# Pairing attention pieces across block edges in a fused retention + feed-forward kernel

## The chip, the cores and the metric

The kernel runs on one core of one Trainium2 chip. The metric is device microseconds (us) of one execution, lower is better. The engines are TensorE (PE, with its weight loads shown as PEld), VectorE (DVE), ScalarE (ACT), GpSimd (POOL) and SyncE (SP); POOL and SP also issue the DMAs that matter here.

## The reference

Eight batches of eight heads, 576 positions, 64 features per head. For every head, scores = q k^T / 8 are multiplied by a decay, gamma^(i-j) for i >= j and 0 above the diagonal, and then by v. The result, laid out as x of 4608 tokens by 512 features, goes through a feed-forward layer:

```python
ret = scores * Dmat[None, :, :, :]
x = np.matmul(ret, v).transpose(0, 2, 1, 3).reshape(B * S, H * D)
h = x @ w_in                       # 512 -> 2048
g = h * np.clip(h + 3.0, 0.0, 6.0) / 6.0
return (g @ w_out).astype(np.float32)   # 2048 -> 512
```

## The kernel before

**Tokens and blocks.** The 4608 tokens are handled as nine blocks of 512 tokens (kb = 0 to 8). Blocks 0 to 7 hold the first 512 positions of one batch each; block 8 holds the last 64 positions of all eight batches. The attention is computed in 36 pieces of 128 tokens: four "main" pieces per batch, and four "rest" pieces (numbers 12, 21, 30 and 35), each made of the 64 last positions of two batches. Pieces 8 to 11 belong to block 2, 13 to 16 to block 3, 17 to 20 to block 4, 22 to 25 to block 5, 26 to 29 to block 6, 31 to 34 to block 7.

**Feed-forward.** For each block, GEMM1 (`gemm1`, matmuls on L400 into `ph`) runs 16 units of four 128x512 matmuls; each unit's result goes through one ACT instruction (L407) and one DVE instruction (L408) into `gt`. GEMM2 (`unit2`, `g2`, L458 into `pout`) then runs 16 units of four matmuls: four token rows (mc) of four units (part). After a row's last unit ACT copies `pout` out (L462) and SP stores it.

**Attention.** It is retention in chunks. For a piece c: `transpose_k` (L286) and `transpose_q` (L291 scales q and v on DVE, L292) make `qk_c` and `vs_c` by DMA transposes on SP's queue. `scores` or `scores_second` multiply k by q on PE (L301, L572); DVE masks the result into `at_c` (L305, L580). `inter` (L323) multiplies q by the running state `tbd`; the first piece of a batch has none. `intra` (L334) adds `at_c` times v; ACT casts the sum into the feed-forward input `xt16` (L340). `update_mm` (L358) forms the piece's contribution to the state, DVE adds and scales it (L371, L374, L375), and ACT copies it into a `tbd` buffer (L387, L388). Rest pieces only read states and update none.

**Steps.** From piece 8 on, the attention is dropped into GEMM2 by hand. `step(ended, begun)` (L585) ends the pieces of one pair (inter, intra) and begins the next pair (scores, update). Its PE order is: inter of both ended pieces, scores of both begun ones, intra of both ended ones, state updates of both begun ones. `put` (L604) runs the units in order and calls whatever stands at unit j after it; j = -1 is ahead of unit 0. During GEMM2 of block kb the pieces of block kb+1 are computed, and those of block kb+2 are transposed (`ahead`, L560). A step also asks for the loads of the pieces six further on (`load_until`; `kn` and `qv` have six buffers), on POOL's queue.

Before the change, the table `AT` (L646) places the steps, and every block starts and ends its own chain of pairs: the first step of a GEMM2 has nothing to end and the last one nothing to begin. A block of four pieces has 3 steps, one of five has 4 (the fifth piece is alone), and block 8's single piece has 2. `ahead` stands at the last four or five units of GEMM2.

**Order and buffers.** The order on each engine is the order of the code. PSUM has 8 banks: four of tag `ph` (shared by GEMM1's `ph`, GEMM2's `pout`, the second scores' two banks and the second inter's `o`), two of `sc`, one of `o` and one of `tu` (state updates). `qk` and `vs` have six buffers each, `at` four, `tbd` five.

Of the kernel before, what the change touches and what calls it, by code (L numbers as in the profile page):

```python
# [11 lines left out]
FP16 = mybir.dt.float16  # L12
# [5 lines left out]
def kernel(  # L18
# [17 lines left out]
    B, H, S, D = q.shape  # L36
    NTOK, DM = out.shape
    DFF = moe_w_in.shape[1]
    P = 128
    NPAIR = H // 2  # L40
# [4 lines left out]
    NMB = NTOK // MBLK  # L45
# [8 lines left out]
    last_of = {}  # L54
    for b in range(B):
# [3 lines left out]
        if b >= 2 and b % 2 == 0 or b == B - 1:  # L59
            j = (b - 1) // 2  # L60
            pieces.append(("rest", j, 0, [(0, 2 * j, MAIN, HALF), (HALF, 2 * j + 1, MAIN, HALF)]))
    last_of[B] = len(pieces) - 1
    NP = len(pieces)
# [9 lines left out]
    work = ctx.enter_context(tc.tile_pool(name="work", bufs=3))  # L73
# [115 lines left out]
    st = {}  # L189
# [7 lines left out]
                later.pop(0)()  # L197

    def scale_v(c):
        vs = work.tile([P, 2, H, D], FP16, tag="vs", bufs=6, name=f"vs_{c}")  # L200
        st.setdefault(c, {})["vs"] = vs[:, 1]
        nc.vector.tensor_tensor(out=vs[:, 1], in0=loaded[c]["qv"][:, 1], in1=gqv[:, 1],  # L202
                                op=ALU.mult)

    def qk_of(c):
        if "qk" not in st.setdefault(c, {}):
            st[c]["qk"] = work.tile([P, 2, NPAIR, P], FP16, tag="qk", bufs=6, name=f"qk_{c}")
        return st[c]["qk"]

    def k_by_pe(c, tag="ph"):  # L210
        kn = loaded[c]["kn"]
        pk = psum.tile([P, NPAIR, P], FP16, tag=tag, bufs=4 if tag == "ph" else 1,
                       name=f"trk_{c}")
        for p in range(NPAIR):
            nc.tensor.transpose(pk[:, p, :], kn[:, 2 * p:2 * p + 2, :], ident16)
        nc.scalar.copy(qk_of(c)[:, 1], pk)  # L216

    def q_by_pe(c):
        q16, qk = loaded[c]["q16"], qk_of(c)
        pq = psum.tile([P, NPAIR, P], FP32, tag="ph", bufs=4, name=f"trq_{c}")  # L220
        for p in range(NPAIR):
            for h2 in range(2):
                r = slice(h2 * HALF, h2 * HALF + HALF)
                nc.tensor.matmul(pq[r, p, :], q16[:, 2 * p + h2, :], dq[:, 2 * p + h2, :],
                                 start=(p == 0), stop=(p == NPAIR - 1), skip_group_check=True)
        if c == EARLY - 1:
            for p in (0, 2):
                nc.scalar.copy(qk[:, 0, p:p + 2], pq[:, p:p + 2])
        else:
            nc.scalar.copy(qk[:, 0], pq)  # L230
# [54 lines left out]
    def transpose_k(c):  # L285
        nc.sync.dma_start_transpose(qk_of(c)[:, 1], loaded[c]["kn"].rearrange("s h d -> s (h d)"))  # L286

    def transpose_q(c):
        vs = work.tile([P, 2, H, D], FP16, tag="vs", bufs=6, name=f"vs_{c}")
        st[c]["vs"] = vs[:, 1]  # L290
        nc.vector.tensor_tensor(out=vs, in0=loaded[c]["qv"], in1=gqv, op=ALU.mult)  # L291
        nc.sync.dma_start_transpose(st[c]["qk"][:, 0], vs[:, 0].rearrange("s h d -> s (h d)"))  # L292
# [126 lines left out]
    def g1_columns(kb, fc, ph, cols):  # L419

        t0 = kb * MBLK
        for dmc in range(NCC):
            nc.tensor.matmul(ph[:, cols], win16[:, dmc, P * fc:P * fc + P],  # L423
                             xt16[:, dmc, t0 + cols.start:t0 + cols.stop],
                             start=(cols.start == 0 and dmc == 0),
                             stop=(cols.stop == MBLK and dmc == NCC - 1),
                             skip_group_check=True)
        if cols.stop == MBLK:
            g1_act(kb, ph, fc)

    def g1_first(kb):

        banks = [g1_bank(kb, fc) for fc in range(2)]
        for dmcs in ((0, 1), (2, 3)):
            for fc in range(2):
                g1_mm(kb, banks[fc], fc, dmcs)
        for fc in range(2):
            g1_act(kb, banks[fc], fc)
# [48 lines left out]
    for i in range(4):  # L487
        if i == 2:
            load(4)
        load_wout(4 * i, 4 * i + 4)  # L490

    scale_v(0)
    for c in range(EARLY):
        k_by_pe(c)
        warm(1, MBLK)
        if c == 0:
            fill_gfull()
        q_by_pe(c)
        if c == 0:
            warm(1, MBLK)  # L500
        else:
            inter(c - 1)
            intra(c - 1)
        if c < EARLY - 1:
            scores(c)
            run_later(9)
            state_early(c)
            run_later(9)
            scale_v(c + 1)
        else:  # L510
            scores_last(c)
            state_early(c)
            out_last(c)
# [9 lines left out]
    def unit1(kb, f0):  # L523
        return lambda: g1(kb, f0)

    def unit2(kb, mc, part):
        return lambda: g2(kb, mc, part)

    def first_step(c):


        old, new, b = c - 1 >= EARLY, c + 1 < 8, pieces[c - 1][1]
        if old:
            before = state_of.get(b)
            o = psum.tile([P, NPAIR, P], FP32, tag="o", name=f"o_{c - 1}")
            st[c - 1].update(o=o, first=True)
            copy = intra(c - 1, copy_later=True, more=before is not None)
            update_mm([c - 1])
            load_until(c - 1 + NBUF)
            update_state(c - 1, copies_later=True)  # L540
        if new:
            q_by_pe(c + 1)
        if old and new:
            run_later(9)
        if EARLY <= c < 8:
            scores(c, 0)
        if old and before is not None:
            for p in range(NPAIR):
                nc.tensor.matmul(o[:, p, :], tbd[before][:, p, :], st[c - 1]["qk"][:, 0, p, :],
                                 start=False, stop=(p == NPAIR - 1), skip_group_check=True)  # L550
        if new:
            k_by_pe(c + 1, "ph" if old else "tu")
        if old:
            copy()
        if c < 8:
            run_later(9)
        if EARLY <= c < 8:
            scale_v(c)

    def ahead(c):  # L560
        transpose_k(c)
        transpose_q(c)
# [41 lines left out]
    def put(units, steps):  # L604

        for do, *which in steps.get(-1, ()):
            do(*which)
        for j, unit in enumerate(units):
            unit()
            run_later(1)  # L610
            for do, *which in steps.get(j, ()):
                do(*which)

    def of_block(kb):
        return list(range(last_of[kb - 1] + 1, last_of[kb] + 1)) if kb < NMB else []

    def gemm1(kb, steps):

        units = {0: [lambda: g1_first(kb)]}.get(kb, [])
        done = {0: 2, 1: 4}.get(kb, 0)  # L620
        put(units + [unit1(kb, f) for f in range(done, NFC)], steps)
# [13 lines left out]
    for fc in range(2):  # L635
        g1_columns(1, fc, banks[fc], done)
    first_step(8)
    transpose_q(8)
    for fc, cols in ((2, done), (0, last), (1, last), (3, done), (2, last), (3, last)):
        g1_columns(1, fc, banks[fc], cols)  # L640
    gts.pop(0)


    gemm1(1, {0: [(transpose_q, 9)], 1: [(transpose_k, 10)],
              4: [(transpose_q, 10)], 5: [(transpose_k, 11)], 8: [(transpose_q, 11)]})
    AT = {1: (-1, 7), 4: (-1, 7, 12), 5: (-1, 3, 7, 11)}  # L646
    for kb in range(1, NMB - 1):
        mine, next_ = of_block(kb + 1), of_block(kb + 2)
        pairs = [mine[i:i + 2] for i in range(0, len(mine), 2)]
        steps = {}  # L650
        for j, ended, begun in zip(AT[len(mine)], [[]] + pairs, pairs + [[]]):
            steps.setdefault(j, []).append((step, ended, begun))
        for j, c in enumerate(next_, start=16 - len(next_)):
            steps.setdefault(j, []).append((ahead, c))
        put([unit2(kb, mc, part) for mc in range(MBLK // P) for part in range(4)], steps)
        gts.pop(kb)
        gemm1(kb + 1, {})
# [34 lines left out]
```

## Time and profile before

| | us |
|---|---|
| median of three runs (308.92 to 309.75) | 309.16 |
| the profiled execution's own time | 308.84 |
| its span (first to last instruction) | 307.0 |
| PE busy in the span | 298.3 (97%) |
| DVE busy | 185.8 (61%) |
| ACT busy | 174.7 (57%) |
| POOL busy | 107.9 (35%) |

The profile is one execution. The chain of waits follows the work that ended last back through whatever released each piece of it; its list in order of time gives the start, the length and the instruction group of each stretch. A stretch's length there runs to the start of the next one, so lengths add up. Timelines of one engine instead give each group's own duration, in which pipelined instructions overlap a little. Times are us from the start of the span. The granted TensorE clock was 0.998 of full speed.

### The profile page before, as it was taken

What the parts mean: (1) busy time and instruction counts of PE and PEld (TensorE: products, weight loads), DVE (VectorE), ACT (ScalarE), POOL (GpSimd) and SP (SyncE); (2) the same over time, 40 slices, a digit from 0 to 9 for tenths busy, and PEclk for the clock granted to TensorE, in tenths of its full rate; (3) what the DMA queues carried; (4) which work ended last, traced back from release to release, by engine and by line L of the source; (5) the groups of instructions that cost most, each with busy time, mean ns of one, the idle gap of its engine ahead of it and who ended that gap; (6) DMA issues with size and microseconds to landing.
All of it is one profiled execution on the core that took longest, in us unless ns stands there. A gap on an engine that the chain in (4) does not pass through costs nothing.

```text
span 307.0 us, 5776 instructions
## 1 busy us (share of the span) xinstructions
PE 298.3 (97%) x2239; PEld 150.1 (49%) x2239; DVE 185.8 (61%) x309; ACT 174.7 (57%) x301; POOL 107.9 (35%) x134
## 2 busy tenths in 40 slices
PE   6999998999999999999999999999999999999994
PEld 2654455544544554445545544455445544444443
DVE  4768336795858872885587738856787357207700
ACT  5568346783667455744574638544765467228611
POOL 8963577636630590055233830257000000000000
PEclk9999999999999999999999999999999999999999
DMA  9999999999999899659999996099920120010022
GB/s 68 147 200 205 190 167 204 169 132 153 158 160 165 85 137 157 106 35 161 167 137 94 139 184 136 4 166 140 141 70 36 68 68 2 34 68 36 1 68 68
DMA packets 153163, 35.51 MB, mean 116 GB/s; under 512 B 143792, under 2 KB 148656, under 8 KB 153136
## 3 DMA queue, kind: packets, MB, share of 16 engines
q0 software_dynamic: 117264, 18.36, 84.6%
q1 hardware_dynamic: 35472, 16.26, 25.7%
q10 hardware_dynamic: 400, 0.52, 0.5%
q8 instruction: 17, 0.28, 0.4%
q14 instruction: 10, 0.08, 0.1%
HBM read 36.70 MB, written 9.44 MB: 150 GB/s over the span
## 4 chain that ended last, share of the span: by engine, by line
PE 83%; DMA 8%; POOL 5%; ACT 2%; DVE 1%; issue 0%; POOLq 0%; ACTq 0%
PE pout L458 37%; PE ph L400 35%; DMA wout<-in_moe_w_out_dram 4%; DMA qv<-in_q_dram 4%; PE o L334 3%; POOL qv L91 2%; PE sc L301 2%; PE o L323 2%; PE u L358 1%; POOL kn L91 1%; POOL win L95 1%; PE pout L471 1%; PE sc L572 1%; PE ph L423 1%; ACT qk L216 0%
## 5 line engine op out<-in xcount | busy, mean ns | idle before, releaser
L408 DVE SCALAR_TENSOR_TENSOR gt<-u,ph 128x512 f16<-128x512 f32 x144 | 98.1, 688 | 63.6 <-ACT u L407 62.9
L458 PE MATMUL pout<-wout,gt 128*128 128x512 f16 x560 | 126.0, 379 | 0.0
L400 PE MATMUL ph<-xt,win 128*128 128x512 f16 x560 | 122.3, 379 | 0.2 <-DVE gt L408 0.2
L407 ACT ACTIVATE u<-ph,cb 128x512 f32<-128x512 f32 x144 | 98.3, 688 | 25.4 <-PE ph L400 24.2
L400 PEld LDWEIGHTS <-win 128*128 128x128 f16 x560 | 54.7, 98 | 66.0 <-issue 0.4
L458 PEld LDWEIGHTS <-gt 128*128 128x128 f16 x560 | 52.7, 98 | 60.8
L91 POOL DMA_DIRECT2D kn<-in_k_dram x40 | 34.5, 865 | 91.8 <-PE u L358 72.6
L462 ACT COPY osb<-pout 128x512 f32<-128x512 f32 x35 | 20.5, 587 | 48.9 <-PE pout L458 48.5
L305 DVE TENSOR_TENSOR at<-sc,mask_wide 128x1024 f16<-128x1024 f32 x19 | 23.2, 1223 | 27.6 <-PE sc L301 27.4
L91 POOL DMA_DIRECT2D qv<-in_q_dram x40 | 34.2, 861 | 6.4 <-DMA wout<-in_moe_w_out_dram 3.3
L91 POOL DMA_DIRECT2D qv<-in_v_dram x40 | 34.6, 870 | 2.8 <-DMA wout<-in_moe_w_out_dram 1.7
L387 ACT COPY tbd<-ts 64x256 f16<-64x256 f16 x28 | 11.4, 406 | 32.7 <-DVE ts L371 16.9
L340 ACT CAST xt<-o 128x512 f16<-128x512 f32 x35 | 19.4, 589 | 6.4 <-PE o L334 4.0
L291 DVE TENSOR_TENSOR vs<-qv,gqv 128x1024 f16<-128x1024 f16 x28 | 18.0, 686 | 3.3 <-DMA qv<-in_v_dram 3.3
L580 DVE TENSOR_TENSOR at<-sc,mask_wide 128x512 f16<-128x512 f32 x24 | 15.4, 682 | 0.0
L334 PE MATMUL o<-at,vs 128*64 128x128 f16 x280 | 12.4, 225 | 1.1 <-ACT xt L340 1.0
L388 ACT COPY tbd<-ts 64x256 f16<-64x256 f16 x28 | 11.3, 403 | 0.4
L334 PEld LDWEIGHTS <-vs 128*64 128x64 f16 x280 | 8.9, 111 | 4.4 <-DVE vs L202 2.1
L374 DVE TENSOR_TENSOR ta<-u,ts 128x256 f32<-128x256 f32 x21 | 8.8, 417 | 3.1 <-PE u L358 3.1
L375 DVE TENSOR_TENSOR ts<-ta,gc 128x256 f16<-128x256 f32 x21 | 8.9, 426 | 1.7
L301 PE MATMUL sc<-qk 64*128 64x128 f16 x184 | 9.6, 226 | 0.4 <-ACT qk L230 0.3
L323 PEld LDWEIGHTS <-tbd 128*128 128x128 f16 x112 | 7.0, 98 | 4.0
(69 smaller groups left out, 117.7 us busy)
## 6 DMA issues: line engine op xcount, KB each, us to landing
out_dram<-osb SPq DMA_DIRECT2D x32, 256.0 KB, 4.1
kn<-in_k_dram POOLq DMA_DIRECT2D x32, 128.0 KB, 4.6
qv<-in_q_dram POOLq DMA_DIRECT2D x32, 128.0 KB, 5.0
qv<-in_v_dram POOLq DMA_DIRECT2D x32, 128.0 KB, 5.7
wout<-in_moe_w_out_dram POOLq DMA_DIRECT2D x4, 512.0 KB, 15.4
win<-in_moe_w_in_dram POOLq DMA_DIRECT2D x3, 512.0 KB, 10.1
win<-in_moe_w_in_dram POOLq DMA_DIRECT2D x2, 256.0 KB, 6.1
kn<-in_k_dram POOLq DMA_DIRECT2D x8, 64.0 KB, 4.5
```

Of the source, the lines that this page charges most:

```text
L91: nc.gpsimd.dma_start(dst[p0:p0 + n], src[b, :, s0:s0 + n, :].rearrange("h s d -> s h d"))
L291: nc.vector.tensor_tensor(out=vs, in0=loaded[c]["qv"], in1=gqv, op=ALU.mult)
L301: nc.tensor.matmul(sc[:, h2, p, :], qk[r, 1, p, :], qk[r, 0, p, :], start=True, stop=True)
L305: later.append(lambda: nc.vector.tensor_tensor(out=at.rearrange("t a b s -> t (a b) s"), in0=sc.rearrange("t a b s -> t (a b) s"), in1=mas ...
L334: nc.tensor.matmul(o[r, p, :], vs[:, 2 * p + h2, :], at[:, h2, p, :], start=(st[c]["first"] and p == 0), stop=(p == NPAIR - 1 and not more ...
L340: nc.scalar.copy(xt16[:, :, g0:g0 + P], o)
L400: nc.tensor.matmul(ph, win16[:, dmc, P * fc:P * fc + P], xt16[:, dmc, t0:t0 + MBLK], start=(dmc == 0), stop=(dmc == NCC - 1))
L407: nc.scalar.activation(u, ph, ACTF.Relu, bias=cb[:, 0:1], scale=1.0 / 6.0)
L408: nc.vector.scalar_tensor_tensor(out=gts[kb][:, fc, :], in0=u, scalar=1.0, in1=ph, op0=ALU.min, op1=ALU.mult)
L458: nc.tensor.matmul(pout, gt[:, fc, P * mc:P * mc + P], wout16[:, fc, :], start=(fc == 0), stop=(fc == NFC - 1))
L462: nc.scalar.copy(osb, pout)
L580: nc.vector.tensor_tensor(out=at[:, h2], in0=banks[h2], in1=mask[:, None, :].to_broadcast([P, NPAIR, P]), op=ALU.mult)
```

## The change

Three things change. First, the pieces from 8 to 35 are paired once for all, (8,9), (10,11), ... (34,35), and a pair may be begun in one block's GEMM2 and ended in the next one's. Only the first step has nothing to end, only the last has nothing to begin, and no piece is alone: 15 steps instead of 23. Second, the places are written out in two tables. `begun_at[kb]` gives unit: pair index; a step at that unit ends the pair before. `ahead_at[kb]` gives unit: piece to transpose. Third, `qk` and `vs` have eight buffers each, since pieces are transposed further ahead. All pieces of a block are still ended before its GEMM1, and block 7's GEMM2 holds no step any more.

```diff
     def scale_v(c):
-        vs = work.tile([P, 2, H, D], FP16, tag="vs", bufs=6, name=f"vs_{c}")
+        vs = work.tile([P, 2, H, D], FP16, tag="vs", bufs=8, name=f"vs_{c}")
...
     def qk_of(c):
         if "qk" not in st.setdefault(c, {}):
-            st[c]["qk"] = work.tile([P, 2, NPAIR, P], FP16, tag="qk", bufs=6, name=f"qk_{c}")
+            st[c]["qk"] = work.tile([P, 2, NPAIR, P], FP16, tag="qk", bufs=8, name=f"qk_{c}")
...
     def transpose_q(c):
-        vs = work.tile([P, 2, H, D], FP16, tag="vs", bufs=6, name=f"vs_{c}")
+        vs = work.tile([P, 2, H, D], FP16, tag="vs", bufs=8, name=f"vs_{c}")
...
-    AT = {1: (-1, 7), 4: (-1, 7, 12), 5: (-1, 3, 7, 11)}
+    pairs = [[c, c + 1] for c in range(8, NP, 2)]
+    begun_at = {1: {-1: 0, 5: 1, 10: 2}, 2: {2: 3, 6: 4, 10: 5}, 3: {3: 6, 10: 7},
+                4: {3: 8, 10: 9}, 5: {3: 10, 10: 11}, 6: {2: 12, 6: 13, 10: 14}, 7: {}}
+
+    ahead_at = {1: {1: 12, 2: 13, 12: 14, 13: 15, 14: 16, 15: 17}, 2: {0: 18, 1: 19, 13: 20, 14: 21},
+                3: {0: 22, 1: 23, 13: 24, 14: 25}, 4: {0: 26, 1: 27, 13: 28, 14: 29},
+                5: {0: 30, 1: 31, 12: 32, 13: 33, 14: 34, 15: 35}, 6: {}, 7: {}}
     for kb in range(1, NMB - 1):
-        mine, next_ = of_block(kb + 1), of_block(kb + 2)
-        pairs = [mine[i:i + 2] for i in range(0, len(mine), 2)]
         steps = {}
-        for j, ended, begun in zip(AT[len(mine)], [[]] + pairs, pairs + [[]]):
-            steps.setdefault(j, []).append((step, ended, begun))
-        for j, c in enumerate(next_, start=16 - len(next_)):
+        for j, i in begun_at[kb].items():
+            steps[j] = [(step, pairs[i - 1] if i else [], pairs[i] if i < len(pairs) else [])]
+        for j, c in ahead_at[kb].items():
             steps.setdefault(j, []).append((ahead, c))
         put([unit2(kb, mc, part) for mc in range(MBLK // P) for part in range(4)], steps)
         gts.pop(kb)
```

More of the change, by code (lines that the diff above doesn't have):

```diff
@@ L612, in put @@
                 do(*which)
-    def of_block(kb):
-        return list(range(last_of[kb - 1] + 1, last_of[kb] + 1)) if kb < NMB else []
     def gemm1(kb, steps):
```

## The prediction

> **What bounds the kernel now.** I read the totals, then the chain of waits, then that chain in order of time. From the page:
>
> ```profile
> span 307.0 us, 5776 instructions
> PE 298.3 (97%) x2239; PEld 150.1 (49%) x2239; DVE 185.8 (61%) x309; ACT 174.7 (57%) x301; POOL 107.9 (35%) x134
> ```
>
> PE is nearly always busy. The chain in order of time says where (start, length, group; here GEMM2 of block 1 with its three steps, the GEMM1 that follows, and the last GEMM2):
>
> ```profile
> 68.57 0.33 PE sc L301 x8
> 68.90 0.22 PE sc L572 x8
> 69.13 0.37 PE u L358 x16
> 69.50 7.01 PE pout L458 x32
> 76.51 0.22 PE o L323 x4
> 76.73 0.33 PE sc L301 x8
> 77.06 0.22 PE sc L572 x8
> 77.29 0.57 PE o L334 x16
> 77.86 0.25 PE u L358 x16
> 78.11 4.42 PE pout L458 x20
> 82.53 0.45 PE o L323 x8
> 82.98 0.57 PE o L334 x16
> 83.54 2.70 PE pout L458 x12
> 86.24 13.81 PE ph L400 x64
> ...
> 289.21 10.36 PE pout L458 x48
> ```
>
> From 58 us to 303 us the chain never leaves PE: steps and GEMMs stand end to end and PE waits for nothing. So whatever PE time a step loses or gains moves the end one for one. Second, changing the kind of matmul costs about 0.11 us. The same eight scores take 0.33 as the first and 0.22 as the second group. Sixteen updates take 0.25 behind intra but 0.37 behind scores. Sixteen GEMM2 matmuls behind a step take 3.56 (elsewhere in this list) against 16 x 10.36 / 48 = 3.45 undisturbed. Only inter, of GEMM2's own shape, starts free (0.22 for four, 0.45 for eight).
>
> **What the steps cost before.** GEMM2 with steps lasts, for blocks 1 to 7, 17.67, 18.68, 17.66, 18.67, 17.67, 18.67 and 14.93 us (start of the first scores to start of the next GEMM1): 123.95. Less seven undisturbed GEMMs of 13.81 (96.67), the 23 steps cost 27.28.
>
> **What they cost after.** Every instruction stays; only the grouping changes. From the rows above: inter 0.22 a piece (rest 0.23; none for 8, 13, 17, 22, 26, 31), scores of a pair 0.55, intra of a pair 0.57, updates of two 0.25, of one (beside a rest piece) 0.12, return to GEMM2 0.11 (7.01 - 32 x 0.2158 = 0.105; 3.56 - 3.45 = 0.107). In order:
> - block 1: 0.92, 1.59, 1.69
> - block 2: 1.60, 1.82, 1.59
> - block 3: 1.69, 1.82
> - block 4: 1.59, 1.82
> - block 5: 1.59, 1.69
> - block 6: 1.60, 1.69, 1.02
>
> This is 23.72, and 15 returns of 0.107 make 25.32. The gain is 27.28 - 25.32 = **1.96 us**. Counted the other way: a begin-only step has three changes of kind, a full one three, an end-only one two, and block 8's first step, with no update, two. That is 61 before and 44 after; 17 at 0.115 is 1.96.
>
> The Trainium skill, "TensorEngine Tiling (Array Packing)", Key Properties, says that a change of tiling mode drains TensorE; these rows agree. It gives no price there. "TensorE: Matmul & The Clock Gate", Step-by-step, puts a drain at about 128 cycles, 53 ns at 2.4 GHz; by that estimate 17 changes would be 0.9 us. The measured 0.11 decides.
>
> **Waits that the new places bring.** I went through each.
>
> *Transposes of piece 13 (block 1, unit 2), the largest unknown.* Pieces 12 and 13 are now transposed in the GEMM2 that also begins them, at unit 10. DVE scales v and q behind the opening step's work; the timelines of DVE, POOL and SP have the three rows that set the pace (start, duration, instruction; the last DVE one of the opening step, the load that the next step lets go, a transpose beside a load):
>
> ```profile
> 73.05 0.43 DVE L375 TENSOR_TENSOR ts<-ta,gc 128x256 f16<-128x256 f32 x1
> 78.28 0.88 POOL L91 DMA_DIRECT2D kn<-in_k_dram  x1 [3.35 <-PE u L358]
> 90.00 1.23 SPq L292 DMA_TRANSPOSE qk<-vs  x1
> ```
>
> The scalings (0.69 each) end at 74.1 and 74.7. SP issues q12, k13, q13 at its pitch of 1.31: 74.1, 75.4, 76.7. PE needs q13 here: opening 0.92 from 68.57, six units 5.29 (six times 0.863 and a return), step 1.59, five units 4.42, inter 0.45 and first scores 0.33 give 81.57. So q13 has 4.85 us to land. This transpose's own view over the kernel:
>
> ```profile
> DMA to landing us min/median/max: 2.4/4.0/8.4
> ```
>
> Pieces 16 and 17 start loading 1.77 us into the unit-5 step (76.51 to 78.28 above), here at 76.6, just as q13 is issued. The row nearest to that is the transpose at 90.00, issued 0.3 us after a load at 89.69: 5.0. The one at 92.69, behind all of that load's issues, took 5.9; the one at 84.64, in a load's tail, 4.8. I take 5.2: wait **0.35**. Ends: 0 (4.85 or less) and 3.6 (8.4, from 56.7 us, while weights were still loading). k13 has 6.1 us (5.9 and 6.9 were its slowest near loads); q12 has 7.1. The load of 16 waits for k12's transpose, long done by 76.6.
>
> *ACT's queue between steps four units apart (blocks 2 and 6, units 2 and 6).* As the changed code hands out the banks, the second scores bank of the step at 6 is `pout` row 0's, so it waits for that row's copy, which ACT runs behind both state copies of the step before. ACT's timeline behind the step that begins pieces 14 and 15, at 104.41 in the chain:
>
> ```profile
> 109.13 0.41 ACT L387 COPY tbd<-ts 64x256 f16<-64x256 f16 x1 [1.24 <-DVE ts L375]
> 109.54 0.40 ACT L388 COPY tbd<-ts 64x256 f16<-64x256 f16 x1
> 109.97 0.59 ACT L462 COPY osb<-pout 128x512 f32<-128x512 f32 x1
> ```
>
> That copy ends 6.15 us after the step began. The new step asks at 1.60 + 3.56 + 0.45 + 0.33 = 5.94. Wait 0.2, twice: **0.4** (0 to 0.6 in all: 0 if the copy's tail overlaps, as on ACT's list, where two copies take 1.07 and not 1.18). What queues behind PE here is the second scores, their masks and the updates; 3.5 us of GEMM2 follow, and the next step is 0.3 us or more later than its inputs.
>
> *Cut off rows of GEMM2.* Steps at 2, 5, 6 and 10 cut a `pout` row, but the next row takes the bank of the second inter: its cast ends 2.2 to 2.45 us after the step began, and PE wants it at 2.56 or later. Price 0; with that cover gone 0.2 each.
>
> *Transposes at units 0 and 1 (blocks 2 to 5).* Their scalings stand behind the last `gt`, to 2.9 us into GEMM2; the fourth transpose is issued at 4.9. Its scores come no earlier than 12.1: 7.2 us, against 2.4 to 6.9 after 83 us. Price 0. Those at units 12 to 15 are used a whole GEMM1 later. SP's stores that stand behind up to eight transposes (10.5 us) hold `osb` buffers not needed for four rows.
>
> *POOL, DVE, buffers.* Loads come as pairs, up to 5.2 us of issue (6.8 with a rest piece), and at least 10 us before the scaling that reads them; the scaling of 17 ends near 88.0, before GEMM1's first `gt` could start at 88.5. More `qk` and `vs` buffers only remove waits, and none on PE shows. At the start of blocks 2 to 7 no step stands between GEMM1 and GEMM2: the last `gt` ends 1.5 us after GEMM1, and GEMM2 reads it after 2.6. Before 58 us nothing moves. All 0.
>
> **Sum.** 308.84 - 1.96 + 0.35 + 0.4 = 307.63 for an execution like the profiled one. That one is 0.32 below the median of 309.16; the same difference of 1.21 gives **307.95**, 0.39% faster. No change can be told from a measurement within 0.3%, 0.93 us, so waits of 1.03 us in all decide between faster and same.
>
> **Rivals.**
> - *No wait shows:* q13 lands in 4.8 as at 84.64 and the copies overlap. 309.16 - 1.96 = 307.2. For: median landing 4.0. Against: loads start just then.
> - *q13 lands late:* 5.9 to 7.3 us (92.69; the transposes around 60 us). Waits 1.05 to 2.45 beside 0.4: 308.65 to 310.05, about no change.
> - *Slower:* q13 meets a backlog like that at 56.7, 8.4 us. 309.16 - 1.96 + 0.4 + 3.55 = 311.15. From 7.4 us on the kernel is slower by 0.3%. For: DMA is over 90% busy until 79 us, and pieces 14 and 15 are still landing. Against: no transpose after 68 us took over 6.9.
> - *The change of kind is not saved:* if it belonged to each group and not to the step, only the 0.75 of waits remains: 309.9. The 0.33 and 0.22 for equal scores speak against it.
>
> **Chances.** Forecast 0.29, no wait 0.22, late q13 0.26, kinds not saved 0.05, slower q13 0.12, and 0.06 for a wait that this trace cannot show, slower too. Faster 0.51, same 0.31, slower 0.18. The range goes from the no-wait case less 0.3 (the 1.96 is a sum of rounded rows), 306.9, to the late case's upper end, 310.0.
>
> **What would show it.** The chain should stay on PE from 58 us, GEMM2 with steps should last near 18.7, 19.3, 17.5, 17.4, 17.3, 18.6 and 13.8 us in blocks 1 to 7, with 13.81 for each GEMM1. PE's waits should name scores behind transposes once (near 81.6) and behind the L462 copy twice. I am wrong if a full step costs more than 1.82, if GEMM1 stretches over 13.81 (DVE held up by a scaling), or if scores wait in blocks 3 to 5.

## The result, and the profile after

The changed kernel is slower. Its median is 313.58 us (five runs, 313.25 to 315.07) against 309.09 for the kernel before, run beside it: a ratio of 1.0152, with a 95% interval of 1.0135 to 1.0170. The forecast was 307.95, with a range of 306.9 to 310.0. The profiled execution took 313.25 us. Single executions over 1.5% above the fastest one of their kernel are left out of every median, spread and ratio in this document.

From the page of the changed kernel, the span, the totals and the row of the granted clock, and below it the row of the clock from the page of the kernel before:

```profile
span 311.4 us, 5772 instructions
PE 297.9 (96%) x2239; PEld 150.5 (48%) x2239; DVE 186.2 (60%) x311; ACT 174.2 (56%) x301; POOL 107.8 (35%) x134
PEclk9799999999979999999999999999999999999999
```

```profile
PEclk9999999999999999999999999999999999999999
```

PE's busy time is 0.4 us less and the span 4.4 us more. The clock row has two dips that the one before does not have. The 7 in the second of its 40 slices stands in the start-up, in code that the change leaves alone; block 1's first step starts 0.29 us later than before, at 68.86. The 7 in the twelfth slice (85.6 to 93.4 us) is the one that matters here. The chain of waits of the changed kernel, in order of time (start, length, group), shows what is ahead of that dip. This is GEMM2 of block 1, as in the forecast's first list:

```profile
68.86 0.33 PE sc L301 x8
...
69.95 5.29 PE pout L458 x24
75.24 0.22 PE o L323 x4
...
76.98 8.27 DMA qk<-vs
85.25 0.14 issue
85.39 0.40 PE sc L572 x8
85.78 0.77 PE o L334 x16
86.55 0.21 PE u L358 x8
86.77 5.75 PE pout L458 x20
92.51 13.81 PE ph L400 x64
```

At 76.98 the chain leaves PE for a DMA: the transpose of q of piece 13 lands 8.27 us after its issue, and the second scores of the step that begins pieces 12 and 13 start only then. PE's own view of its waits has it once:

```profile
PE sc L572 <- DMA qk<-vs: 3.3, 1, 3.3
```

Behind the wait everything on PE is slow as well: five units take 5.75 us instead of 4.42, the intra 0.77 instead of 0.57. The table by windows of the same kernel says why. Each line has the window, its length, the busy time and number of instructions of PE, PEld, DVE, ACT and POOL, and then the granted clock (the number behind POOL's), the DMA share and GB/s; the last two are not used here:

```profile
68.86:85.39 16.53, 13.18 (x146) 7.22 (x146) 11.12 (x19) 6.15 (x13) 13.12 (x15) 1.00 2.16 162
85.39:87.00 1.61, 1.61 (x33) 1.27 (x34) 1.20 (x2) 0.83 (x2) 0.00 (x0) 0.69 1.69 252
87.00:89.00 2.00, 2.00 (x6) 0.76 (x5) 2.00 (x5) 1.43 (x4) 1.93 (x3) 0.50 2.39 158
89.00:92.51 3.51, 3.51 (x17) 1.52 (x15) 0.90 (x2) 0.21 (x1) 0.70 (x1) 0.94 2.43 155
```

The lost clock is 0.31 x 1.61 + 0.50 x 2.00 + 0.06 x 3.51 = 1.7 us. In the kernel before, the same stretch ran at 1.00 throughout.

The stages (start of a GEMM2, or of its first step, to the start of the next GEMM1) put the whole loss in one place:

| block | before | forecast | after |
|---|---|---|---|
| 1 | 17.67 | 18.7 | 23.65 |
| 2 | 18.68 | 19.3 | 19.48 |
| 3 | 17.66 | 17.5 | 17.54 |
| 4 | 18.67 | 17.4 | 17.44 |
| 5 | 17.67 | 17.3 | 17.32 |
| 6 | 18.67 | 18.6 | 18.80 |
| 7 | 14.93 | 13.8 | 13.81 |
| sum | 123.95 | 122.6 | 128.04 |

Blocks 2 to 7 stand within 0.2 us of the forecast. Block 1 is 4.95 above it: some 3.2 more of waiting than the 0.35 that was priced, and 1.7 of clock. With 0.29 more ahead of block 1 the stages make 4.38 of the 4.4 us of span.

**Why the transpose is late: the loads.** On POOL's timeline of the changed kernel the loads of pieces 14, 15, 16, 17 and 18 run on without a gap (one load is three issues, `kn`, q and v; here the end of 15's and the start of 16's, 17's and 18's):

```profile
74.47 0.92 POOL L91 DMA_DIRECT2D qv<-in_v_dram  x1
75.33 0.93 POOL L91 DMA_DIRECT2D kn<-in_k_dram  x1
...
77.93 0.95 POOL L91 DMA_DIRECT2D kn<-in_k_dram  x1
...
80.53 0.97 POOL L91 DMA_DIRECT2D kn<-in_k_dram  x1
```

In the kernel before, the load of 16 waited until 78.28 for the update at unit 7, as a line of the forecast shows, and that of 18 until 89.69 for a transpose, that of k of 12:

```profile
89.69 0.88 POOL L91 DMA_DIRECT2D kn<-in_k_dram  x1 [6.15 <-DMA qk<-kn]
```

The code explains the difference. There are six `kn` buffers, and a buffer comes free with the last reader of its piece. For a main piece that is its state update (L358). Piece 12 is a rest piece and has no update, so its last reader is its transpose. The change moves that transpose from a late unit to unit 1, so the buffer of 12 comes free ahead of those of 10 and 11, and the load of 16 takes it. It does not wait for the unit-5 step at all; 17 then takes 10's and 18 takes 11's. The loads slow each other as well: those issued from 75 to 84 us need a median of 9.0 us to land, those issued ahead of them, from 70 to 75 us, 5.0.

### The profile page after: what moved, and what is told of

Its sections match the earlier page's. It is cut to its first block, busy times and chain, and to the rows that moved or that the text cites. A ratio compares the mean times of both kernels' runs of the same rounds, so it can differ in the third digit from the quotient of the medians.

```text
span 311.4 us, 5772 instructions
## 1 busy us (share of the span) xinstructions
PE 297.9 (96%) x2239; PEld 150.5 (48%) x2239; DVE 186.2 (60%) x311; ACT 174.2 (56%) x301; POOL 107.8 (35%) x134
## 4 chain that ended last, share of the span: by engine, by line
PE 83%; DMA 6%; POOL 4%; ACT 3%; DVE 2%; issue 1%; POOLq 0%; ACTq 0%
PE ph L400 38%; PE pout L458 35%; DMA win<-in_moe_w_in_dram 3%; PE o L334 3%; DMA qk<-vs 3%; POOL qv L91 2%; PE sc L301 1%; POOL kn L91 1%; PE o L323 1%; PE pout L471 1%; PE sc L572 1%; PE u L358 1%; DVE at L580 1%; PE ph L423 1%; DVE ts L375 1%
## 5 line engine op out<-in xcount | busy, mean ns | idle before, releaser
L458 PEld LDWEIGHTS <-gt 128*128 128x128 f16 x560 | 53.7, 98 | 63.0 <-issue 1.8
L387 ACT COPY tbd<-ts 64x256 f16<-64x256 f16 x28 | 11.3, 404 | 18.7 <-DVE ts L375 14.3
L291 DVE TENSOR_TENSOR vs<-qv,gqv 128x1024 f16<-128x1024 f16 x28 | 18.1, 684 | 0.0
L580 DVE TENSOR_TENSOR at<-sc,mask_wide 128x512 f16<-128x512 f32 x24 | 15.4, 681 | 2.5 <-PE sc L572 2.5
L334 PE MATMUL o<-at,vs 128*64 128x128 f16 x280 | 12.2, 227 | 1.1 <-ACT xt L340 0.9
L572 PE MATMUL sc<-qk 64*128 64x128 f16 x112 | 5.9, 216 | 3.6 <-DMA qk<-vs 3.3
L301 PE MATMUL sc<-qk 64*128 64x128 f16 x168 | 8.6, 222 | 0.5 <-ACT qk L230 0.5
```

The lines of the kernel that those rows point to most:

```text
L334: nc.tensor.matmul(o[r, p, :], vs[:, 2 * p + h2, :], at[:, h2, p, :], start=(st[c]["first"] and p == 0), stop=(p == NPAIR - 1 and not more ...
L458: nc.tensor.matmul(pout, gt[:, fc, P * mc:P * mc + P], wout16[:, fc, :], start=(fc == 0), stop=(fc == NFC - 1))
L580: nc.vector.tensor_tensor(out=at[:, h2], in0=banks[h2], in1=mask[:, None, :].to_broadcast([P, NPAIR, P]), op=ALU.mult)
```

## The experiments

The theory after this reading: the early transpose of the rest piece frees a `kn` buffer, so three more loads follow without a gap, and the backlog delays what is needed soon. One rival is that the transposes themselves queue (three in a row, the third always late); another, that the loads don't matter and it is the place of the step.

**1. The order of the two transposes swapped** (`e1_swap`, and `e8_swap_look`, one more execution of the same kernel, whose profile is read here).

```diff
-    ahead_at = {1: {1: 12, 2: 13, 12: 14, ...
+    ahead_at = {1: {1: 13, 2: 12, 12: 14, ...
```

> The changed kernel with the transposes of piece 13 at unit 1 and those of piece 12 at unit 2, in this order. Traffic theory: q13 landed 8.3 us after its issue, and not 5.2, because the early transpose of the rest piece 12 freed its k buffer, so that the load of 16 followed that of 15 without a gap (75.33 us) and five loads ran in a row. Swapped, 16 can't start before the transpose of k12 has landed (about 80.5), so the last transpose (q12, issued near 77) lands in 5 to 6 us, and PE waits 0.5 to 1.5 us with little loss of clock: 308.5 to 309.8. Queue theory: a transpose that stands behind three others on SP's queue lands in 8 us whatever the loads do: q12 lands at 85.3, wanted at 81.4: a wait of 3.9, and as much lost clock as now: 313.6 to 314.5.

> The swapped transposes once more, for an undisturbed profile, since they came out slower than the changed kernel and neither theory said so for a landing time of 5 to 6 us. If q12 is the late one: PE's wait list names scores of 12 behind its transpose, 3 us or more, and the load of 16 starts only after k12 has landed. If the late loads hold DVE instead: GEMM1 of block 2 stretches over 13.81 us by 2 us or more, with its first unit behind the scaling of 16 or 17.

Measured: 315.10 us (three runs, 314.86 to 316.09; ratio 1.0213, 1.0191 to 1.0235), and 316.32 for the execution of `e8_swap_look`. That is above the ranges of both theories. PE waits only 0.8 us for the transposes there, but 5.3 us in GEMM1 of block 2. The chain of `e8_swap_look` in order of time:

```profile
75.46 6.21 DMA qk<-kn
...
82.20 0.86 POOL kn L91
...
86.52 8.41 DMA qv<-in_v_dram
...
95.01 0.69 DVE vs L291
95.70 0.61 DVE gt L408
...
96.35 13.05 PE ph L400 x48
```

Read downwards: the load of 16 again takes 12's buffer, and starts when 12's transpose, now the later one, has landed (82.20). The load of 17, behind it, lands at 94.93. The scaling of 17, placed at unit 15, stands on DVE ahead of GEMM1's first results (`gt`), so GEMM1 stops. So moving the release of this one buffer later made the opposite mistake, and the same loads held another engine.

On the transposes themselves this trace decides between the two theories. No load starts between 74.92 and 82.20, and q of 12, now the last of the three and issued at 76.80, lands in 5.2 us. The queue theory wanted 8 us whatever the loads do; it falls.

**2. Loads of 16 and 17 held back** (`e2_hold`): they are asked for behind unit 9, and a one-column read of 12's `kn` on DVE keeps that buffer busy until then, so that 16 takes the buffer of 10 as it did before.

```diff
-            load_until(c + NBUF)
+            load_until(15 if begun == [10, 11] else c + NBUF)
...
+    def hold():
+        nc.vector.tensor_copy(kept, loaded[12]["kn"][:, 0, 0:1])
+        load_until(17)
...
+        if kb == 1:
+            steps.setdefault(9, []).append((hold,))
```

> The changed kernel with loads 16 and 17 asked for after unit 9 of block 1, behind one small DVE read of k12, so that 16 takes the buffer of 10 and 17 that of 11, as before the change; 16 starts at 76.6 us and not at 75.3, as the prediction assumed. If the 1.3 us without a gap are what made the backlog, q13 lands in 5 to 6 us: 308.2 to 309.3. If loads that run beside the transposes make it, whichever starts them, q13 still lands in 7 to 8.3 us and PE waits 2 to 3.4 us: 311.5 to 313.5.

Measured: 309.80 us (309.50 to 311.73, ten runs; the profile is that of the 311.73), ratio 1.0033 (1.0017 to 1.0050). POOL's timeline of this kernel has the start of the load of 16, and its chain the transpose of q of 13:

```profile
77.01 0.88 POOL L91 DMA_DIRECT2D kn<-in_k_dram  x1 [1.63 <-PE u L359]
```

```profile
77.13 6.65 DMA qk<-vs
...
83.92 0.55 PE sc L573 x8
```

With a gap of 1.6 us in the loads the transpose takes 6.65 us in place of 8.27, and 3.6 of the 4.5 us are gone (each kernel against the one before that ran beside it). This is the strongest single piece of evidence for the buffer. It is between the two ranges expected, because even this transpose is slower than the 5.2 of the forecast; PE still waits 1.6 us for it.

**3. The step three units later** (`e3_unit13`).

```diff
-    begun_at = {1: {-1: 0, 5: 1, 10: 2}, ...
+    begun_at = {1: {-1: 0, 5: 1, 13: 2}, ...
```

> The changed kernel with the step that begins 12 and 13 after unit 13 of block 1 and not after unit 10: three units, 2.6 us, more for the transposes. If the whole loss is PE's wait for q13 and the clock lost behind it, a wait of 0.5 to 1 us and a full clock remain: 308.5 to 309.3. If steps of two full pairs in a cut row cost it in themselves, the time stays near 313.

Measured: 310.43 us (309.99 to 314.02, eight runs), ratio 1.0052 (1.0017 to 1.0088); the profile is that of the 309.99. The wait for the transpose falls from 3.3 to 0.9 us, but a wait in GEMM1 of block 2 appears. PE's waits, and then the chain, of this kernel:

```profile
PE sc L572 <- DMA qk<-vs: 0.9, 1, 0.9
PE ph L400 <- DVE gt L408: 1.6, 2, 1.4
```

```profile
78.11 11.05 DMA qv<-in_q_dram
89.16 2.06 issue
91.22 0.69 DVE vs L291
91.92 0.61 DVE gt L408
```

The q half of the load of 17 needs 11.05 us to land. The v half, issued behind it at 78.98, needs 12.2 and lands at 91.2, which is where the list has its 2.06 of `issue`; the scaling reads both, and it holds the first `gt`. The step's place is not the cause, it only chooses which consumer of the backlog waits.

**4. The early transposes alone** (`e4_early12`): the kernel before, with only 12 and 13 transposed behind units 1 and 2 of block 1.

```diff
-        for j, c in enumerate(next_, start=16 - len(next_)):
+        for j, c in zip((1, 2, 13, 14, 15) if kb == 1 else range(16 - len(next_), 16), next_):
```

> The kernel before, with only the transposes of 12 and 13 moved from units 11 and 12 of block 1 to units 1 and 2. Nothing reads them before 100 us. Both theories: the time stays (308.8 to 309.4). Traffic theory: the loads of 16 to 18 move ahead, and q13 lands 7 to 8.5 us after its issue. If q13 lands in 5 us here, what slowed it in the changed kernel lies in the pairing or the buffers and not in the early transposes.

Measured: 309.35 us (308.91 to 311.04, eleven runs; the profile is that of the 311.04), ratio 1.0015 (1.0001 to 1.0028). Two rows of POOL's timeline, and the view of the transpose of q of 13, issued at 78.93:

```profile
76.20 0.92 POOL L91 DMA_DIRECT2D qv<-in_v_dram  x1
77.06 0.93 POOL L91 DMA_DIRECT2D kn<-in_k_dram  x1
```

```profile
DMA to landing us min/median/max: 7.8/7.8/7.8
```

The load of 16 follows that of 15 without a gap, and the transpose needs 7.8 us; the four that the kernel before issues from 84.6 to 92.7 us need 3.2 to 5.9. So two moved transposes are enough to make the backlog, without pairs across edges or more buffers. It costs next to nothing here because nothing reads q of 13 until the next GEMM2.

**5. No load beside the transpose at all** (`e5_gate`): three one-column DVE operations hold all three buffers until q of 13 has landed, and 16 and 17 are scaled and transposed in GEMM1 of block 2.

```diff
-            load_until(c + NBUF)
+            load_until(15 if begun == [10, 11] else c + NBUF)
...
+    def gate():
+        for c in (12, 10, 11):
+            nc.vector.tensor_tensor(out=kept, in0=loaded[c]["kn"][:, 0, 0:1],
+                                    in1=st[13]["qk"][:, 0, 0, 0:1], op=ALU.mult)
+        load_until(17)
...
-    ahead_at = {1: {1: 12, 2: 13, 12: 14, 13: 15, 14: 16, 15: 17}, 2: ...
+    ahead_at = {1: {1: 12, 2: 13, 12: 14, 13: 15}, 2: ...
...
+        if kb == 1:
+            steps[9] = [(gate,)]
...
+        gemm1(kb + 1, {5: [(ahead, 16)], 8: [(ahead, 17)]} if kb == 1 else {})
```

> The changed kernel with the loads of 16, 17 and 18 held by three one-column DVE reads until q13's transpose has landed, and the scalings and transposes of 16 and 17 moved from units 14 and 15 of block 1's GEMM2 to units 5 and 8 of the next GEMM1, so that the late loads hold nobody. Traffic theory: with only the tail of 14 and 15 beside it, q13 lands in 4 to 5.5 us, PE waits at most 0.7 us and keeps its clock; the 5.3 us lost in block 1's GEMM2 go: 308.0 to 309.0. If the transposes are late for any other reason, the wait stays 3 us or more: 312.5 to 314.

Measured: five runs scatter from 308.34 to 312.59, median 310.69; the ratio of 1.0033 has an interval of 1.0000 to 1.0066. As a time it settles nothing. Its profiled execution (309.60 us) shows the two rows that were wanted. The chain:

```profile
76.46 6.11 DMA qk<-vs
...
92.64 11.44 DMA qv<-in_v_dram
```

With the load of 16 held until 83.12, q of 13 still takes 6.11, more than the 4 to 5.5 expected: the loads of 14 and 15, issued up to 75.6, are enough for that, beside the two transposes ahead of it and the store of an output row behind it, which all these kernels have. PE waits 0.5 us for it. The loads that were held then come in a bunch of four (16 to 19). The last piece of them, issued at 92.64, lands 12.5 us later, at 105.1 (the list above breaks off its stretch at 104.09, where DVE's instruction before ends). DVE, which has the scaling of 19 next, stands idle for 1.16 us up to 105.25; the masks and state work of a step are behind that scaling, and the next step's second scores wait 0.7 us for ACT instead of some 0.35.

The same transpose, issued at 76.46 to 77.13 in these three, takes longer the earlier the load of 16 starts:

| kernel | load of 16 starts | landing of q of 13 |
|---|---|---|
| changed | 75.33 | 8.27 |
| loads held | 77.01 | 6.65 |
| gate | 83.12 | 6.11 |

Three more kernels leave these loads as the changed one has them, and q of 13 took 8.3 (`e3_unit13`), 8.1 (`e7_space`) and 8.6 us (`e11_bufs6`) in them. So the early load is worth more than the scatter. A landing by itself does scatter: the transpose of q of 12, two issues ahead, took 5.3 in the changed kernel, 7.3 with the loads held and 5.7 with the gate. So the shares of the 8.27 us can't be told apart closer than that.

**6. Steps of blocks 2 and 6 five units apart** (`e7_space`), the second disputed cost.

```diff
-    begun_at = {..., 2: {2: 3, 6: 4, 10: 5}, ... 6: {2: 12, 6: 13, 10: 14}, 7: {}}
+    begun_at = {..., 2: {2: 3, 7: 4, 12: 5}, ... 6: {2: 12, 7: 13, 12: 14}, 7: {}}
```

> The changed kernel with the steps of blocks 2 and 6 at units 2, 7 and 12 in place of 2, 6 and 10, so that the row copy that the second scores' bank waits for is done. Copy theory: GEMM2 of blocks 2 and 6 lasts 19.14 and 18.44 and not 19.48 and 18.80; the kernel is 0.7 us faster than the changed one (312.5 to 313.2), with block 1 as it was. If those 0.35 us are not that wait, no difference in these two stages.

Measured: 313.12 us (four runs, 311.98 to 313.78); block 2 lasts 19.15 and block 6 18.45, each 0.33 to 0.35 less than in the changed kernel, whose chain shows what has gone (the copy of a `pout` row on ACT, then the second scores of the step at unit 6):

```profile
114.40 0.59 ACT osb L462
115.00 0.04 issue
115.04 0.38 PE sc L572 x7
```

The wait for the copy was real, 0.35 each time. Block 1 keeps its wait (3.3 us) here.

**7. Block 1 as before, pairs across edges from piece 18 on** (`e6_mixed`): 17 steps and 48 changes of matmul kind.

```diff
-    begun_at = {1: {-1: 0, 5: 1, 10: 2}, 2: {2: 3, 6: 4, 10: 5}, 3: {3: 6, 10: 7}, ...
+    steps_at = {1: {-1: ([], 0), 7: (0, 1), 12: (1, [])},
+                2: {-1: ([], 2), 3: (2, 3), 7: (3, 4), 11: (4, [])},
+                3: {-1: ([], 5), 5: (5, 6), 10: (6, 7)},
+                4: {3: (7, 8), 10: (8, 9)}, 5: {3: (9, 10), 10: (10, 11)},
+                6: {2: (11, 12), 7: (12, 13), 12: (13, [])}, 7: {}}
...
-    ahead_at = {1: {1: 12, 2: 13, 12: 14, 13: 15, 14: 16, 15: 17}, 2: {0: 18, 1: 19, 13: 20, 14: 21},
+    ahead_at = {1: {11: 12, 12: 13, 13: 14, 14: 15, 15: 16}, 2: {0: 17, 12: 18, 13: 19, 14: 20, 15: 21},
```

> The steps of the kernel before in block 1's GEMM2 (at -1, 7 and 12, 12 to 16 transposed at units 11 to 15), and pairs across the edges from 18 on: 17 steps, 48 changes of matmul kind against 61 before and 44 in the changed kernel; steps in blocks 2, 3 and 6 placed so that no bank waits for a copy. If a change of kind costs 0.115 us and nothing waits: 13 x 0.115 = 1.5 us below the kernel before, 307.3 to 307.8. If pairing over the edges costs something by itself, no faster than 308.9.

Measured: 310.05 us (308.48 to 311.86, ten runs), ratio 1.0031 (1.0009 to 1.0052): not faster. Block 1 lasts 17.86, so its wait is gone, but block 3 takes 20.90. The chain there has the pattern again, at another step (the one behind unit 10, which begins 22 and 23):

```profile
142.43 6.54 DMA qk<-vs
...
149.10 0.40 PE sc L572 x8
```

Piece 23 is transposed behind unit 1, the opening step's two loads are issued until 140.2, and the step behind unit 5 lets another go at 142.09, 0.34 us before this transpose is issued. PE waits 2.1 us. That leaves a test with a number:

**8. The same, with the steps of block 3 two units later** (`e9_late_step`).

```diff
-                3: {-1: ([], 5), 5: (5, 6), 10: (6, 7)},
+                3: {-1: ([], 5), 7: (5, 6), 12: (6, 7)},
```

> The mixed version again (block 1 grouped as before, pairs across edges from piece 18 on), with block 3's second and third step two units later, behind units 7 and 12. In the mixed version block 3 lasted 20.90 us: the transpose of q of piece 23, issued at 142.43, took 6.54 us and its scores waited 2.1. Two units later those scores come 1.73 us later, and the step's loads start some 1.4 us after that transpose is issued instead of 0.3 ahead of it. Theory (a transpose is late when fresh loads start beside it): the wait is at most 0.4 us, block 3 lasts 17.7 to 18.1 us, and 48 changes of matmul kind against 61 show: 13 x 0.115 = 1.5 us below the kernel before run beside it, 1.0 to 1.6 with the rest of the wait. Rival (what the transposes cost only moves to another place, as in the kernel with the gate): block 3 as short, but a wait of 1 us or more in block 4 or in a GEMM1, and a time within 0.5 us of the kernel before.

Measured: 307.53 us (306.90 to 307.80, six runs) against 309.07 beside it, ratio 0.9935 (0.9912 to 0.9958). This beats both kernels. From 58 us on the chain of waits stays on PE as it did before. Around the step of block 3 that had waited it reads:

```profile
141.41 0.45 PE o L323 x8
...
143.10 4.42 PE pout L458 x20
147.52 0.46 PE o L323 x12
```

The 1.54 us between the medians agrees with the 13 x 0.115 = 1.5 of the saved changes (the ratio's interval, 1.3 to 2.7 us, holds both); in the profiled execution (307.80, the highest of the six) the stages of blocks 1 to 7 sum to 122.57 against 123.95, 1.38 less. Block 3 lasts 18.57, not the 17.7 to 18.1 that was expected: its steps (0.92, 1.69 and 1.83), three returns of 0.107 and 13.81 make 18.57 with no wait at all, so that length was added up wrongly, and nothing was lost. The rival, that the cost only moves on, does not hold here.

The transpose itself is faster here, too: q of 23, issued at 143.03, lands in 3.8 us and not in 6.54. But the reason given in the expectation is not what the rows show. The next load starts 0.4 us behind that transpose, and not 1.4; what differs is the pause in the loads ahead of it, 3.58 us here and 1.89 in the mixed version:

```profile
143.40 0.88 POOL L91 DMA_DIRECT2D kn<-in_k_dram  x1 [3.58 <-PE u L358]
```

**9. The buffers, alone and taken away** (`e10_bufs8_alone`: the kernel before with eight `qk` and `vs` buffers; `e11_bufs6`: the changed kernel with six).

```diff
-        vs = work.tile([P, 2, H, D], FP16, tag="vs", bufs=6, name=f"vs_{c}")
+        vs = work.tile([P, 2, H, D], FP16, tag="vs", bufs=8, name=f"vs_{c}")
...
-            st[c]["qk"] = work.tile([P, 2, NPAIR, P], FP16, tag="qk", bufs=6, name=f"qk_{c}")
+            st[c]["qk"] = work.tile([P, 2, NPAIR, P], FP16, tag="qk", bufs=8, name=f"qk_{c}")
```

(The other kernel has the same lines the other way round.)

> The kernel before with eight qk and vs buffers in place of six, nothing else. The order on every engine is the same. Theory (buffers were waited for by nobody): the time of the kernel before run beside it, within 0.3%, and transposes issued at the same times in GEMM2 of block 1 (from 84.6 us on). Rival (the buffers themselves move transposes or put them elsewhere in memory at a price): over 0.3% off, with transposes at other times or PE waits on qk that the kernel before does not have.

> The changed kernel with six qk and vs buffers again. Piece 18's buffers are then piece 12's, which the step behind unit 2 of block 2 frees with its intra, near 110.8 us; the scalings of 18 and 19 stand ahead of that step's masks and state work on DVE and would end near 112.1 instead of 109.2. Theory (the eight buffers are needed by the transposes at units 0 and 1, in block 2 alone): block 1 as in the changed kernel (3.3 us wait for q13), block 2's masks and states 2.4 us late, its GEMM2 1.5 to 3 us longer than 19.48, PE waiting in it for DVE or ACT work, the other blocks unchanged: 315 to 317 us. Rival (six would have done): block 2 within 0.3 us of 19.48 and the time within 0.5 us of the changed kernel's 313.6.

Measured: the buffers alone 309.16 us, ratio 1.0004 (0.9983 to 1.0025), transposes in GEMM2 of block 1 from 84.32 on in place of 83.27, and GEMM1 behind them from 87.30 in place of 86.24, so later by as much: no change. The changed kernel with six buffers takes 317.06 us, ratio 1.025 (1.022 to 1.028). Its GEMM2 of block 2 lasts 22.80 us instead of 19.48, a little more than expected; blocks 3 to 6 are unchanged. PE waits 1.8 us there for the copy of a `pout` row on ACT, in place of 0.35, and behind that wait the granted clock falls again (0.71, 0.50 and 0.93 in the three windows of 2 us from 117 to 123), which loses another 1.7 us. DVE's timeline there shows the scalings of 18 and 19 waiting for the intra of 12, and the masks behind them:

```profile
110.87 1.29 DVE L291 TENSOR_TENSOR vs<-qv,gqv 128x1024 f16<-128x1024 f16 x2 [2.32 <-PE o L334]
112.08 1.22 DVE L305 TENSOR_TENSOR at<-sc,mask_wide 128x1024 f16<-128x1024 f32 x1
```

So the eight buffers are what lets the early transposes of block 2 run; by themselves they are worth nothing, and they don't cause the loss.

## Why the prediction was wrong

**The saved changes of kind: right.** Blocks 3, 4, 5 and 7, in which nothing waits, last 17.54, 17.44, 17.32 and 13.81 against 17.5, 17.4, 17.3 and 13.8. Blocks 2 and 6 without the ACT wait last 19.15 and 18.45 in the sixth experiment, and the forecast's steps and returns sum to 19.14 and 18.44 without it. The version with 13 fewer changes is 1.54 us faster where 1.5 was worked out. The rival that the changes are not saved falls.

**The step that failed: the wait for the transposes of piece 13.** It was priced at 0.35 us and cost about 5.3: 3.5 of waiting (PE would have asked at 81.57, 0.29 later with the later start, and began at 85.39; the view of PE's waits has 3.3 of it) and 1.7 to 1.8 of clock. Three things went into it.
- *The start of the load of 16.* The forecast took 76.6, from the row where an update lets the load go, and set the wait on 12's transpose aside as "long done by 76.6". It was done, but that was all the load needed: it took 12's buffer and started at 75.33, with two more loads queued behind it. The second and fourth experiment show it; by the second it is worth about 8.27 - 6.65 = 1.6 us of landing.
- *The landing beside loads.* With the load where the forecast had it (77.01), the transpose still took 6.65, not 5.2. The row at 90.00 that gave 5.0 came 0.3 us behind a single load that followed a pause of 6.15 us; here six issues of the pieces 14 and 15 stood directly ahead. The gate's 6.11 shows that they were enough without a later load. This is about 1.45 us more.
- *The clock.* The forecast had no term for it, in any case or rival. An end of 3.6 us for the wait was given, and the time at that end should have been 309.16 - 1.96 + 0.4 + 3.55 = 311.15. From there to the 313.58 measured it is 2.4 us: 1.7 of clock, 0.3 of later start and 0.3 of the copies on ACT.

The issue times of the three transposes, by contrast, were right: 74.39, 75.68 and 76.98 against 74.1, 75.4 and 76.7, the difference being the start of the block.

**The slower rival was the right mechanism**, a backlog like that around 56.7 us, and had 0.12. The forecast set its row of 8.4 us aside as one from a time when weights were still loading. That reading was wrong: the last load of weights was issued at 24.48 and landed 15.4 us later, near 40. What ran around 56.7 us were loads of pieces, from 52.08 to 60.78 with no pause over 1.3 us, which took 6.9 to 10.6 us to land. So that row came from just the traffic that the change was to make at 77 us. The row against it, "no transpose after 68 us took over 6.9", was a row of a kernel whose loads had gaps of 3.35 and 6.15 us; the change removed these gaps.

**The copies on ACT: right in kind, short in size.** 0.35 each instead of 0.2, 0.3 us in all.

**The loads, priced at zero.** The forecast looked at how far ahead of its reader each load comes, and found 10 us enough. In the changed kernel that held, but with the step later or the transposes swapped a load of 17 landed after 12.2 us or started 7 us late, and stopped GEMM1 through DVE. The zero was luck of the place, not a margin.

**Cut rows, transposes at units 0 and 1, the buffers: right**, nothing waits for them in blocks 2 to 6; but the last experiment shows that the buffers are needed in block 2, where six of them cost 3.3 us more, half of it clock.

## What to carry to other kernels

When an operation moves, ask of each buffer it reads whether it is the last reader; if it is, the move also moves the load that waits for the buffer, and everything queued behind that load. The landing time of a transfer is no property of the transfer: take it from a row with the same traffic ahead of it, and if the change itself alters that traffic, give the range of the worst stretch. A forecast wait of some microseconds on the matmul engine needs a term for the clock behind it (1.7 us each behind the waits of 3.3, 1.6 and 1.8 us here, and none behind one of 2.1).

## What the runs showed of the hardware

A DMA transpose that needs 2.4 us at best took 6.1 behind two loads, 6.65 with a third starting beside it, and 8.1 to 8.6 with loads running on without a gap (8.27 in the changed kernel, 8.3, 8.1 and 8.6 in three more). The loads went from 4.4 us (median, kernel before, issued from 70 to 84 us) to 9.0 (changed kernel, 75 to 84 us), and single ones to 15.5 (`e3_unit13`, issued at 82.36).

After the 3.3 us wait the granted clock was 0.50 for some 2 us and partly on either side, which adds up to 1.7 / 0.5 = 3.4 us at half rate, if all that was lost was lost at half rate. The Trainium skill, "TensorE: Matmul & The Clock Gate", "What's actually happening", tells of a free-running window of about 3.4 us and of half the clock after an idle one; the length at half rate agrees. The length of the idle time does not: with the loads held, a wait of 1.6 us was enough, and with six buffers one of 1.8 us. The windows of the kernel with the loads held:

```profile
83.90:85.70 1.80, 1.78 (x33) 1.54 (x34) 1.24 (x2) 0.63 (x2) 0.99 (x2) 0.54 2.33 162
85.70:88.00 2.30, 2.30 (x7) 0.82 (x7) 2.27 (x5) 1.73 (x4) 2.03 (x3) 0.62 1.99 219
```

while 2.1 us in the mixed version left the clock at 1.00, as the windows of that one show:

```profile
148.50:150.30 1.80, 1.20 (x41) 1.09 (x42) 0.00 (x0) 0.42 (x1) 0.00 (x0) 1.00 1.39 301
150.30:152.50 2.20, 2.20 (x13) 1.02 (x12) 1.97 (x5) 1.46 (x4) 2.01 (x3) 1.00 0.36 29
```

What decides between them stays open; no run was made for it. A wait of 1.6 us is less than half of 3.4, so a window that is idle throughout can't be what lowered the clock there.
